# Loading all of w4 as one tile over 16 DMA engines, in place of 128 rows apart, in a decode kernel of attention and MLP

## The chip, the cores, the metric

One core of one Trainium2 chip. The metric is the device time of one execution in microseconds (us); most fast runs of one kernel lie within about 0.3% of each other. A trace of one profiled execution stands beside the times; its span is the time from the first to the last instruction, about 1.8 us less than the time.

## The reference

One decode step for 4 batch entries: attention of 32 query heads over the last 2048 entries of a cache with 16 key/value heads, plus a small MLP, added up.

```python
q = (xn @ wq)                       # [4, 32 heads, 128]
scores = einsum(q, K window) / sqrt(128); p = softmax(scores); o = p @ V window
attention = o @ wo                  # [4, 576]
h2 = gelu(layernorm(x1) @ w3) @ w4  # w3: [576, 4608], w4: [4608, 576]
out = x + attention + x1 + h2
```

K and V windows are 16 x 2 MB each, the weights some 20 MB more: 87 MB are read for an output of 4.5 KB.

## The kernel before

SyncE issues all large loads in one fixed order into one queue. K and V share six buffers; w4 has the buffer of wq and w3. The kernel before holds 35 of 36 w4 rows of each partition in a tile and brings the last 128 rows apart, in eight small loads whose shapes are chosen so that they go to few DMA engines.

```python
NFM = NF - 1                                   # 35
W4_PIECES = [0, NFH, NFM - 11, NFM - 6, NFM - 2, NFM - 1, NFM]
def load_w4():
    t = wp.tile([P, NFM, D], BF16, tag="w", name="w4_sb")
    for lo, hi in zip(W4_PIECES, W4_PIECES[1:]):
        ...
        nc.sync.dma_start(out=t[:, lo:hi, :], in_=src[:, lo - e * NFH:hi - e * NFH, :])

def x4_rows(part):
    t = w_tiles["x4"]                          # a buffer of the K and V pool
    if part == "A":                            # 100 rows: 5 shares of 4 partitions x 5 rows
        src = B_w4[X0 + 28:F, :].rearrange("(q g i) n -> g q (i n)", q=4, g=5)
        nc.sync.dma_start(out=t[0:NX, XA * D:XS * D], in_=src)
    elif part == "C":                          # 12 rows: 3 shares of 4
        ...
    else:                                      # B, 16 rows in six loads of one partition each
        ...
X_AFTER = {13: ["A", (0, 0, 4)], 14: [(1, 0, 4), (2, 0, 2), "C"], 15: [(2, 2, 4), (3, 0, 2), (3, 2, 4)]}
...
order = [("K", 0), ("K", 1), ("K", 2)]         # then V0, K3, V1, K4 ... V13, X, V14, V15; then w4
def flush_loads():                             # issues the next loads while buffers are free
    ...
            if kind == "X" or kind == "V" and h > min(X_AFTER):
                for part in X_AFTER.get(h, []):
                    x4_rows(part)
...
mlp_extra(XC, XS)                              # 12 + 8 matmuls on the rows apart, near the end
...
for lo, hi in pieces:
    mlp_out(lo, hi)                            # two matmuls for each row of the tile
```

## Time and profile before

| | before |
|---|---|
| time, fast runs of the first two series | 211.12 to 211.66 us |
| span of the profiled execution | 209.6 us |
| read from memory | 87.17 MB |
| last completion of V15 / of w4 | 194.51 / 206.60 us |
| first of w4's sixteen completions | 204.81 us |

A load over 16 DMA engines is complete when all sixteen have reported. The trace holds each report, so each load has sixteen completion times, without the number of the engine. They are given below as sorted lists. "Late" is an engine that has been set back by some 1.3 us against the others, "half-late" one that has been set back by some 0.5 to 0.9 us.

### The profile page before, as it was taken

To read this page: it belongs to the slowest core of one execution; us is meant where nothing else is said; L and a number is where in the kernel's file an instruction comes from. 1 tells how busy PE (TensorE), PEld (TensorE's weight loads), DVE (VectorE), ACT (ScalarE), POOL (GpSimd) and SP (SyncE) were. 2 spreads that over 40 slices of the span, in tenths; PEclk is the share of its full clock that TensorE was granted. 3 is DMA by queue.
4 is the path that set the end of the run, shared out by engine and by line. 5 is a ranking of instruction groups with operands and counts; after the bars stand their busy time and mean duration, and the time that the engine had idled before them with its cause. 6 is when DMAs were issued, how large, how long until landed. Compare 5 with 4: busy or idle time off the path is not lost.

```text
span 209.6 us, 2356 instructions
## 1 busy us (share of the span) xinstructions
PE 150.2 (72%) x958; PEld 58.2 (28%) x972; DVE 113.4 (54%) x156; ACT 34.8 (17%) x72; POOL 9.0 (4%) x32
## 2 busy tenths in 40 slices
PE   0357297699590039958998987589697955999693
PEld 0122132233140003213444332234232312343361
DVE  4511877894910083935608889176848390764200
ACT  7612201012010011110222221102111111023100
POOL 4710000000000000000002100000000000000000
PEclk9999589999787555788999999789978796699979
DMA  7999999999999999999999999999999999999992
GB/s 301 400 419 425 425 424 430 438 432 424 434 450 406 427 435 420 443 428 435 428 428 435 419 428 434 435 425 438 428 428 438 415 439 435 416 441 428 432 403 98
DMA packets 6702, 87.31 MB, mean 417 GB/s; under 512 B 758, under 2 KB 1034, under 8 KB 1700
## 3 DMA queue, kind: packets, MB, share of 16 engines
q1 hardware_dynamic: 6684, 87.17, 97.7%
q8 instruction: 7, 0.11, 0.2%
q10 hardware_dynamic: 8, 0.00, 0.0%
q14 instruction: 3, 0.02, 0.0%
HBM read 87.17 MB, written 0.00 MB: 416 GB/s over the span
## 4 chain that ended last, share of the span: by engine, by line
DMA 66%; DVE 15%; PE 14%; ACT 1%; issue 1%; SPq 1%; DVEq 0%; ACTq 0%
DMA kn<-in_A_k_cache_dram 43%; DVE kt L253 12%; DMA vn<-in_A_v_cache_dram 10%; DMA w_sb<-in_B_w_dram 7%; DMA wq_sb<-in_A_wq_dram 6%; PE S L366 5%; PE g_ps L496 2%; PE q_ps L310 2%; PE O L423 1%; PE oT L436 1%; DVE PT L400 1%; PE acc L212 1%; DVE mx L372 1%; PE S L388 1%; ACT E L395 1%
## 5 line engine op out<-in xcount | busy, mean ns | idle before, releaser
L366 PE MATMUL S<-kt,qz 128*128 128x512 bf16 x242 | 76.4, 437 | 32.2 <-DVE kt L253 30.4
L253 DVE STREAM_TRANSPOSE kt<-kn 128x2048 int32<-128x2048 int32 x32 | 73.4, 2297 | 24.3 <-DMA kn<-in_A_k_cache_dram 22.9
L366 PEld LDWEIGHTS <-qz 128*128 128x128 bf16 x256 | 23.5, 106 | 64.3 <-issue 47.7
L423 PE MATMUL O<-vn,PT 128*32 128x512 bf16 x256 | 23.9, 414 | 9.3 <-DMA vn<-in_A_v_cache_dram 9.3
L430 ACT ACTIVATE O_sb<-O,rd 128x512 f32<-128x512 f32 x16 | 11.0, 686 | 64.7 <-DVE rd L413 48.3
L395 ACT ACTIVATE E<-S 128x512 bf16<-128x512 f32 x16 | 9.5, 597 | 72.6 <-PE S L388 72.6
L400 DVE STREAM_TRANSPOSE PT<-E 128x512 bf16<-128x512 bf16 x16 | 11.4, 710 | 14.4 <-ACT E L395 14.4
L446 DVE TENSOR_REDUCE on<-oT 128x8 bf16<-128x128 f32 x16 | 4.6, 289 | 22.1 <-PE oT L436 21.9
L423 PEld LDWEIGHTS <-PT 128*32 128x32 bf16 x256 | 5.5, 95 | 33.0 <-issue 22.1
L436 PE MATMUL oT<-ident_w,O_sb 128*128 128x128 f32 x64 | 12.7, 331 | 0.3 <-ACT O_sb L430 0.3
L372 DVE TENSOR_REDUCE mx<-S 128x1 f32<-128x512 f32 x16 | 10.5, 659 | 1.1 <-PE S L366 1.1
L436 PEld LDWEIGHTS oT<-ident_w,O_sb 128*128 128x128 f32 x64 | 8.3, 165 | 5.2 <-issue 4.3
L388 PE MATMUL S<-nm,j_row 8*128 8x512 bf16 x16 | 6.7, 421 | 1.8 <-DVE nm L384 1.7
L354 PE MATMUL S<-negbig,ohT 4*128 4x512 bf16 x16 | 6.2, 384 | 0.0
L212 PE MATMUL acc<-w_sb,gT 128*4 128x288 bf16 x70 | 5.5, 311 | 0.6 <-DMA w_sb<-in_B_w_dram 0.6
L310 PE MATMUL q_ps<-wq_sb,xnT 128*32 128x512 bf16 x40 | 4.3, 611 | 2.2 <-DMA wq_sb<-in_A_wq_dram 2.2
L212 PE MATMUL acc<-wo_sb,op 128*4 128x288 bf16 x64 | 5.5, 324 | 0.4 <-DVE op L468 0.4
L496 PE MATMUL g_ps<-w_sb,ln2T 128*32 128x512 bf16 (+2 forms) x55 | 5.5, 441 | 0.0
L212 PEld LDWEIGHTS <-gT 128*4 128x4 bf16 (+3 forms) x90 | 4.2, 89 | 3.1 <-issue 1.0
L538 POOL TENSOR_TENSOR g_u<-g_x 128x180 f32<-128x180 f32 x1 | 0.5, 486 | 101.9 <-ACT g_x L532 101.9
L681 DVE CAST fin<-acc 4x288 bf16<-4x288 f32 x1 | 0.4, 446 | 8.1 <-PE acc L212 8.1
L534 DVE COPY g_x<-gT_ps 128x64 f32<-128x64 f32 x2 | 0.4, 223 | 7.5 <-PE gT_ps L518 7.5
(94 smaller groups left out, 79.3 us busy)
## 6 DMA issues: line engine op xcount, KB each, us to landing
kn<-in_A_k_cache_dram SPq DMA_DIRECT2D x16, 2048.0 KB, 25.9
vn<-in_A_v_cache_dram SPq DMA_DIRECT2D x16, 2048.0 KB, 22.7
wo_sb<-in_A_wo_dram SPq DMA_DIRECT2D x4, 1152.0 KB, 37.8
w_sb<-in_B_w_dram SPq DMA_DIRECT2D x1, 4608.0 KB
wq_sb<-in_A_wq_dram SPq DMA_DIRECT2D x1, 4096.0 KB
w_sb<-in_B_w_dram SPq DMA_DIRECT2D x1, 2592.0 KB, 11.0
w_sb<-in_B_w_dram SPq DMA_DIRECT2D x2, 576.0 KB, 34.3
w_sb<-in_B_w_dram SPq DMA_DIRECT2D x1, 864.0 KB
```

The lines of the kernel that those rows point to most:

```text
L212: nc.tensor.matmul(out=acc_of(i), lhsT=lhsT, rhs=rhs[:, i * CW:(i + 1) * CW], start=False, stop=False, skip_group_check=True)
L253: nc.vector.transpose(out=kt[:], in_=src)
L310: nc.tensor.matmul(out=q_ps[r][g * QD:(g + 1) * QD, :], lhsT=xnT[:, k, :], rhs=wq_sb[:, col:col + NW], start=(j == 0), stop=False, skip_gr ...
L366: nc.tensor.matmul(out=S_ps[h][:], lhsT=qz[:, z0:z0 + P], rhs=kt[:, ib, c0:c0 + SC, e:2 * QD:2].rearrange("p c k -> p (c k)"), start=False ...
L372: nc.vector.reduce_max(out=mx[:], in_=S_ps[h][:], axis=AX.X)
L388: nc.tensor.matmul(out=S_ps[h][:], lhsT=j_row[:], rhs=st.pop(("nm", h))[:, 0:1].to_broadcast([NJ, NW]), start=False, stop=False, skip_grou ...
L395: nc.scalar.activation(out=E[h][:].rearrange("p c k -> p (c k)"), in_=S_ps.pop(h)[:], func=ACT.Exp, scale=scale, accum_out=st["rs"][:, h % ...
L400: nc.vector.transpose(out=PT[h][:], in_=E.pop(h)[:])
L423: nc.tensor.matmul(out=O_ps[h][g * QD:(g + 1) * QD], lhsT=PT[h][:, c, :], rhs=vn[:, :, c, :], start=(s == 0), stop=False, skip_group_check ...
L430: nc.scalar.activation(out=O_sb[h][:], in_=O_ps.pop(h)[:], func=ACT.Copy, scale=st.pop(("rd", h)))
L436: nc.tensor.transpose(out=oT[:, s, :], in_=o[:, s, :], identity=ident_w[:, s * NJ:s * NJ + P])
L496: nc.tensor.matmul(out=out, lhsT=ln2T[:, k, :], rhs=rhs, start=(j == 0), stop=False, skip_group_check=True)
```

## The change

It drops the loads apart and all that serves them, for a simpler kernel: one tile of 36 rows, the usual 16 engines, no matmuls on four, twelve or twenty partitions, no reordering of the MLP's columns.

```diff
-    NFM = NF - 1
-    W4_PIECES = [0, NFH, NFM - 11, NFM - 6, NFM - 2, NFM - 1, NFM]
+    W4_PIECES = [0, NFH, NF - 12, NF - 6, NF - 2, NF - 1, NF]
     def load_w4():
-        t = wp.tile([P, NFM, D], BF16, tag="w", name="w4_sb")
+        t = wp.tile([P, NF, D], BF16, tag="w", name="w4_sb")
...
-    def x4_rows(part):
-        ... (parts A, B and C)
-    X_AFTER = {13: ["A", (0, 0, 4)], ...}
...
     # in mlp_g, told in words: out go the matmuls on the 128 columns apart and ACT's copies of them in a new order
     # in mlp_turn, told in words: out go ten transposes and five ACT copies, in comes one DVE copy, as in the other rounds
...
-            if kind == "X":
-                load_x4()
-            else:
-                load_kv(kind, h)
-            ...
+            load_kv(kind, h)
...
-    mlp_extra(XC, XS)
-    mlp_extra(XB, XC)
```

## The prediction

> **What bounds the kernel now.** I read the page's busy slices first, then the chain of waits, then the last 10 us in order of time, then the landing of every transfer. The title of the change also speaks of denominators that two heads share. The kernel before already does that (its step of the denominators returns at even heads), and the diff does not touch it: nothing is counted for it. What changes is w4 alone.
>
> The page, DMA row and rate in 40 slices, and the queue that carries the loads:
> ```profile
> DMA  7999999999999999999999999999999999999992
> GB/s 301 400 419 425 425 424 430 438 432 424 434 450 406 427 435 420 443 428 435 428 428 435 419 428 434 435 425 438 428 428 438 415 439 435 416 441 428 432 403 98
> ...
> q1 hardware_dynamic: 6684, 87.17, 97.7%
> q8 instruction: 7, 0.11, 0.2%
> ```
> All slices but the first and the last are full. 87.17 MB between the first packet (about 1.4 us) and the last landing (206.60 us) are 425 GB/s. Compute shows no such row: PE is busy 72% and DVE 54% of the span.
>
> The end of the chain of waits of the kernel before, and the SyncE issues from 158 us on:
> ```profile
> 167.94 21.71 DMA vn<-in_A_v_cache_dram
> ...
> 191.35 14.53 DMA w_sb<-in_B_w_dram
> 205.88 0.04 issue
> 205.92 1.05 PE acc L212 x12
> 206.97 0.43 DVE fin L681
> ```
> ```profile
> 163.21 0.91 SPq L164 DMA_DIRECT2D x<-in_B_w_dram  x1
> 164.17 0.36 SPq L171 DMA_DIRECT2D x<-in_B_w_dram  x1
> 167.94 0.55 SPq L103 DMA_DIRECT2D vn<-in_A_v_cache_dram  x1
> 168.55 1.91 SPq L171 DMA_DIRECT2D x<-in_B_w_dram  x2
> 175.07 0.82 SPq L167 DMA_DIRECT2D x<-in_B_w_dram  x1
> 179.94 0.56 SPq L103 DMA_DIRECT2D vn<-in_A_v_cache_dram  x1
> 184.76 0.81 SPq L171 DMA_DIRECT2D x<-in_B_w_dram  x3
> 189.67 5.67 SPq L153 DMA_DIRECT2D w_sb<-in_B_w_dram  x6
> ```
> The chain ends with w4's landing, 12 short matmuls, the copy and the store. The 21.71 us on V and the 14.53 us on w4 are mostly queueing: V15, issued at 179.94 us, lands at 194.51, one regular period of 4.86 us after V14 (189.65). Each 2 MB load of K or V lands that far after the one ahead of it through the whole second half. So no issue comes late enough to leave an engine without work, and issuing earlier can gain nothing.
>
> **The sixteen engines apart.** The trace has each engine's completion of each transfer. K2's sixteen lie between 28.23 and 28.74 us. At 30.63 us a packet of 16384 B of the instruction queue runs for 967 ns, and in the next transfer (wo) fifteen engines end between 30.98 and 31.46 us and one at 32.80: 1.34 us behind the next to last. It never catches up; V0 has it at 37.66, K3 at 42.50. Six more such packets come at 64.8, 105.2, 121.7, 147.0, 179.1 and 198.7 us, and after each of those I can follow one more engine is late. V12 ends on eleven engines at 173.14 to 173.97 and on five at 174.60 to 175.06.
>
> The kernel before uses this. It takes the last 128 rows of w4 out of the tile (35 rows instead of 36 for a partition) and loads them apart: part A completes on 5 engines (183.75 to 184.56 us), part C on 3, each of the six pieces of B on one. After the first of these, V14 shows five engines at 187.83 to 188.17 and the rest up to 189.65; at the end w4 has four at 204.81 to 205.14 and twelve at 205.91 to 206.60. Late engines and laden engines were made to end together. They are different engines: a late one with part A's 20 rows on top would have landed V15 about 0.9 us after 194.51, and none does.
>
> **What the Trainium skill says.** "DMA: Bandwidth & Descriptors", section "Why a DMA increments its semaphore by 16 and not by 1": a transfer from SyncE runs on the largest number of engines up to 16 that divides the slowest dimension of both sides, and on the lowest-numbered ones. The trace agrees on the number (5, 3 and 1 completions for slowest dimensions of 5, 3 and 1); which engines they are it cannot show. The same page, "Where 436 GB/s comes from", puts the ceiling at 435 GB/s; the 425 here is close to it, the rest being the imbalance at the end and the start. "Runtime: NRT & Kernel Launch", section "Instruction fetch mechanics": instructions are refilled in 16 KiB blocks, at a cost it calls "mostly hidden". The trace shows the 16384 B packets, hidden from the compute engine indeed, but costing one DMA engine 1.34 us that it never makes up.
>
> **The change, part by part.**
>
> Transfers: removed are eight small loads (2.2 to 112.5 KB, 147,456 B together); added is one row for each partition in the tile, the same 147,456 B over all sixteen engines, 8 rows or 9,216 B each. Per engine this is: one engine loses 40 rows and gains 8, two lose 24, two lose 20, and eleven only gain 8. The last late engine is among those eleven. It took from 194.51 (V15) to 206.60 us for 280 rows of 1152 B, or 322,560 B in 12.09 us, 26.7 GB/s. The 9,216 B more take 9,216 / 26.7 GB/s = 0.345 us (the single-row pieces of w4, 8 rows on an engine, landed 0.36 us apart, 206.24 and 206.60, which agrees). Hence w4's last landing goes from 206.60 to about 206.95 us. This lies wholly on the path that sets the end. The other term, the relief of five engines by 12 to 32 rows (0.5 to 1.4 us), is worth nothing, for nobody waits for them.
>
> PE: 20 short matmuls on x (12 at 193.02 for 0.90 us, 8 at 197.86 for 0.65 us) go, and two on the tile's extra row come, some 0.16 us by the 78 ns spacing of the 58 at 200.78 (4.53 / 58). The 12 run while V15 is awaited (194.65), the 8 beside the DVE pair of mk and op (197.97 to 198.85); neither is on the path. The 2 more fall into the 0.61 us in which PE waited for w4 before 205.92. After the last landing the same two matmuls, copy and store remain: 0 us.
>
> PE, ACT, POOL in the MLP stage at 98 to 116 us: five matmuls, ten transposes and about eight small ACT copies go, one DVE copy of some 0.2 us (223 ns for its larger kin) comes. The loads of that stage kept their 4.85 us period, so this is worth 0 us.
>
> SyncE and buffers: x's place in the order of loads and its eight issues go. V14 can take x's place at 163.2 us, V15 that of V14 at 167.9, and w4's pieces follow between 168 and 185 as their semaphores come free, instead of 189.7 to 194.9 us. They only wait longer in the queue: 0 us.
>
> Sum: +0.345 us. The fast times before are 211.28, 211.57 and, profiled, 211.41, mean 211.42. I expect 211.42 + 0.35 = 211.77, and put 211.8.
>
> **The rivals.**
>
> 1. The engines share one limit, so that only bytes count: then 147 KB moved from five engines to sixteen change nothing, +0.0 us, 211.4. For it: the 425 GB/s near the stated ceiling. Against it: the late engine of 30.6 us stays late for over 150 us while the others run on; had they a common limit, slack would be shared out at the end only.
>
> 2. The earlier issue of V14, V15 and w4 and the lost small packets help: -0.3 to -0.5 us, 211.0. For it: the chain names the issues of w4 at 189.67 to 191.35. Against it: 4.86 us between V14 and V15, no gap.
>
> 3. Instruction refills move. Some 66 fewer PE instructions (35 matmuls and transposes with their weight loads, less 4) put the last refills a few us later, the seventh into w4's rows at about 202 us. If each refill keeps its own engine, the one hit then ends below 206.6 us, no harm. If one fell on an engine that is already late, that engine ends 1.34 us later: some 213.1. Against it: seven refills hit seven different engines as far as I can follow them. If one of the late refills disappears, several late engines remain: no gain.
>
> 4. PE becomes the end: rows up to 30 done by about 205.5 us, 0.7 us before they'd be needed at 206.2. A clock lower by a quarter there would use that up and add some 0.5 us.
>
> **Range and chances.** The likely error is run-to-run scatter (0.29 us between the two fast runs) plus rivals 1 and 2 on the low side, 3 and 4 on the high side: 211.3 to 212.6. 2% are 4.2 us, far beyond every term here, the worst being rival 3. Within 2%: 0.98; faster 0.005; slower 0.015.
>
> **What would show it.** In the changed kernel's trace: V14 and V15 with the late engines at the same times as before (189.65 and 194.51) and the gap of five engines at V14 gone, nine to ten engines early instead of five; w4's last completion near 206.95 with nine or so engines at 205.1 to 205.9; the end of the chain again w4, a dozen acc matmuls, fin; issue of w4 before 186 us; the DMA row still full. Wrong would be: last landing at or below 206.6 (rival 1 or 2), an engine some 1.3 us behind all others (rival 3), PE without idle time ahead of its last matmuls (rival 4), or a K or V landing more than 5 us after the one before it, which would mean that compute does reach the queue.

## The result, and the profile after

| | before | after |
|---|---|---|
| median of six runs | 211.50 us | 211.73 us |
| fast runs | 211.12 to 211.66 us | 211.49 to 212.00 us |
| ratio of the fast runs | | 1.0014, 95% interval 1.0000 to 1.0028 |
| span | 209.6 us | 210.0 us |
| last completion of V14, V15 | 189.65, 194.51 us | 189.71, 194.57 us |
| last completion of w4 | 206.60 us | 206.98 us |

One run of the kernel before, of 646.39 us, is among the six of its median and not among the fast ones; the record does not say what it met. A ratio is the mean time of one kernel's fast runs over that of the other's fast runs of the same rounds, so it is not quite the ratio of the medians. 1.0014 of 211.4 us is 0.3 us: same, by any use one could make of it, and at the edge of what six runs resolve. The trace resolves it better.

The page of the kernel after, DMA row, rate and queues:

```profile
DMA  7999999999999999999999999999999999999991
GB/s 300 399 421 431 434 428 428 428 431 438 454 400 421 432 424 426 447 424 424 440 421 434 437 414 438 431 437 428 426 428 434 429 432 434 428 431 437 419 403 61
...
q1 hardware_dynamic: 6632, 87.17, 97.5%
q8 instruction: 7, 0.11, 0.2%
```

The bytes are the same, the row is as full as before, and there are seven refills still (a refill is a packet of the instruction queue, q8, that fetches instructions). The end of its chain of waits, and the issues of SyncE from 155 us on (start us, duration us, what):

```profile
175.13 31.13 DMA w_sb<-in_B_w_dram
206.26 0.04 issue
206.30 1.06 PE acc L181 x12
207.36 0.43 DVE fin L607
```
```profile
157.43 9.99 SPq L103 DMA_DIRECT2D vn<-in_A_v_cache_dram  x3
167.47 17.67 SPq L141 DMA_DIRECT2D w_sb<-in_B_w_dram  x6
207.87 0.35 SPq L610 DMA_DIRECT2D out_dram<-fin  x1
```

The chain has the same four members at its end, 0.38 us later. w4's pieces are now issued between 167.5 and 185.1 us, up to 22 us earlier than before, and they wait the longer: 31.13 us in the chain in place of 14.53. The last matmuls start 0.38 us later (206.30 for 205.92) and the tail after w4's last landing is the same (2.99 us before, 3.03 us after).

The sixteen completions of w4's last piece, in us, from the trace's records:

```
before  204.81 204.96 205.08 205.14 | 205.91 206.16 206.21 206.34 206.36 206.37 206.40 206.42 206.43 206.50 206.51 206.60
after   205.02 205.04 205.08 205.09 205.24 205.25 205.36 205.78 205.98 | 206.49 206.54 206.59 206.61 206.64 206.68 206.98
```

Twelve engines ended together before. Nine engines are early now, and the seven that refills set back end alone, later than before.

### The profile page after: what moved, and what is told of

Same layout as the page of the kernel before. It is cut to its first block, busy times and chain, and to the rows that moved or that the text cites. A ratio compares the mean times of both kernels' runs of the same rounds, so it can differ in the third digit from the quotient of the medians.

```text
span 210.0 us, 2284 instructions
## 1 busy us (share of the span) xinstructions
PE 145.9 (69%) x939; PEld 55.5 (26%) x939; DVE 113.6 (54%) x157; ACT 34.1 (16%) x64; POOL 8.7 (4%) x31
## 4 chain that ended last, share of the span: by engine, by line
DMA 63%; PE 22%; DVE 11%; ACT 1%; issue 1%; SPq 0%; ACTq 0%
DMA vn<-in_A_v_cache_dram 42%; DMA w_sb<-in_B_w_dram 15%; PE S L335 9%; DVE kt L222 9%; DMA wq_sb<-in_A_wq_dram 6%; PE O L392 3%; PE g_ps L457 2%; PE q_ps L279 2%; PE acc L181 1%; PE S L357 1%; PE oT L405 1%; DVE mx L341 1%; ACT E L364 1%; DVE qz L311 1%; PE gT_ps L469 1%
## 5 line engine op out<-in xcount | busy, mean ns | idle before, releaser
L335 PE MATMUL S<-kt,qz 128*128 128x512 bf16 x256 | 77.4, 432 | 33.7 <-DVE kt L222 32.7
L392 PE MATMUL O<-vn,PT 128*32 128x512 bf16 x256 | 23.3, 405 | 11.1 <-DMA vn<-in_A_v_cache_dram 11.1
L405 PE MATMUL oT<-ident_w,O_sb 128*128 128x128 f32 x64 | 11.4, 305 | 0.3 <-ACT O_sb L399 0.3
L405 PEld LDWEIGHTS oT<-ident_w,O_sb 128*128 128x128 f32 x64 | 7.3, 150 | 4.7 <-issue 3.9
L181 PE MATMUL acc<-w_sb,gT 128*4 128x288 bf16 x72 | 5.0, 285 | 2.2 <-DMA w_sb<-in_B_w_dram 2.2
L181 PE MATMUL acc<-wo_sb,op 128*4 128x288 bf16 x64 | 4.6, 286 | 1.0 <-DVE op L437 1.0
L457 PE MATMUL g_ps<-w_sb,ln2T 128*32 128x512 bf16 (+1 forms) x50 | 4.9, 444 | 0.0
L475 DVE COPY g_x<-gT_ps 128x64 f32<-128x64 f32 (+1 forms) x3 | 0.6, 195 | 7.3 <-PE gT_ps L469 7.3
L206 PE MATMUL tp<-ident_bf,first 4*128 4x4 bf16 x8 | 0.6, 173 | 5.5 <-DVE first L193 5.5
## 6 DMA issues: line engine op xcount, KB each, us to landing
vn<-in_A_v_cache_dram SPq DMA_DIRECT2D x16, 2048.0 KB, 26.7
wo_sb<-in_A_wo_dram SPq DMA_DIRECT2D x4, 1152.0 KB, 26.7
```

The costliest lines, as they stand in the source:

```text
L181: nc.tensor.matmul(out=acc_of(i), lhsT=lhsT, rhs=rhs[:, i * CW:(i + 1) * CW], start=False, stop=False, skip_group_check=True)
L335: nc.tensor.matmul(out=S_ps[h][:], lhsT=qz[:, z0:z0 + P], rhs=kt[:, ib, c0:c0 + SC, e:2 * QD:2].rearrange("p c k -> p (c k)"), start=False ...
L392: nc.tensor.matmul(out=O_ps[h][g * QD:(g + 1) * QD], lhsT=PT[h][:, c, :], rhs=vn[:, :, c, :], start=(s == 0), stop=False, skip_group_check ...
L405: nc.tensor.transpose(out=oT[:, s, :], in_=o[:, s, :], identity=ident_w[:, s * NJ:s * NJ + P])
L457: nc.tensor.matmul(out=g_ps[g * QD:(g + 1) * QD], lhsT=ln2T[:, k, :], rhs=rhs, start=(j == 0), stop=False, skip_group_check=True)
```

## The experiments

The theory: each DMA engine works off its own share at its own pace, an engine that fetched instructions stays late for good, and the latest engine sets the end. Rows apart go to engines that have time, so in the tile they cost what they add to the late engines. The main rival: all engines share one limit, and only bytes count.

### Without the rows apart, and with one row less in the tile

Both take 147,456 B away. The first, from the kernel before, takes them off the few engines that carry them; the second, from the kernel after, takes 9,216 B off each of sixteen.

```diff
 # e1_no_rows_apart, on before (wrong on purpose: the matmuls on these rows take rows of wo)
-                for part in X_AFTER.get(h, []):
-                    x4_rows(part)
+                pass
```

> The kernel before, without the eight loads of the rows apart (its matmuls on them stay, on other data, so the result is wrong on purpose). 147,456 B fewer come from memory. My theory (each of the sixteen DMA engines works off its own share, and the engines delayed by instruction refills end last): the engines that carried those rows were not the last, so w4's last completion stays at 206.5 to 206.7 us in the trace and the time stays within 0.1 us of the kernel before. Rival (one common limit, only bytes count): 147,456 B at 425 GB/s are 0.35 us, so the last completion falls to about 206.25 and the time by 0.35 us.

```diff
 # e3_row_35_left_out, on after (wrong on purpose: row 34 used twice)
-    W4_PIECES = [0, NFH, NF - 12, NF - 6, NF - 2, NF - 1, NF]
+    W4_PIECES = [0, NFH, NF - 12, NF - 6, NF - 3, NF - 2, NF - 1]
+    acc_matmuls([(gT[:, NF - 1, :], w_tiles["w4"][:, NF - 2, :])])
```

> The changed kernel with only 35 of the 36 rows of each partition loaded (row 34 is used twice in the products, so the same number of matmuls and a wrong result on purpose). The same 147,456 B fewer, but 9,216 B on each of the sixteen engines. My theory: the last completion of w4 falls by 0.345 us, from 206.98 to about 206.63, and the time by 0.35 us to that of the kernel before. Rival (one common limit): the same 0.35 us; it is the pair with the run without the rows apart that tells the two apart. Rival (the time of the change came from the matmuls or from the order of the loads): nothing changes, 0.0 us.

Measured: the first 211.16 us (ratio to before 0.9986, interval 0.9972 to 0.9999), the second 211.38 us (1.0003, 0.9984 to 1.0021). The second fits the time of the kernel before, as expected, but its interval (0.34 us less to 0.44 us more) would hold the change's 0.3 us as well. The first is at 0.02 to 0.59 us less, an interval that reaches from my "within 0.1" to the rival's 0.35 and beyond. So the times decide neither; the traces do. From V15 to w4 no rows apart are in the queue, and the last engine takes:

| kernel | rows in the tile | last of V15 | last of w4 | between |
|---|---|---|---|---|
| before | 35 | 194.51 | 206.60 | 12.09 |
| e1, no rows apart | 35 | 194.30 | 206.36 | 12.06 |
| e3, row 35 left out | 35 | 194.60 | 206.67 | 12.07 |
| after | 36 | 194.57 | 206.98 | 12.41 |
| e6, empty slot (below) | 36 | 194.50 | 206.87 | 12.37 |
| e7, more PE instructions (below) | 36 | 194.22 | 206.64 | 12.42 |

One row for each partition is 0.33 us, in six executions. For the rows apart one has to look from before they come: the five engines that are late at V12 report at 174.60 to 175.06 us in the kernel before, 174.54 to 174.65 us in e1. The last of them ends w4 31.54 us later in the kernel before (206.60), and in e1 the five end at 206.08 to 206.19 us, 31.54 us later as well; under one limit they'd have 0.35 us less. The mean of the sixteen engines does lose it: from K14 to w4 39.76 us (166.25 to 206.01) before, 39.37 us (166.04 to 205.41) in e1. So the bytes left, and only engines that nobody waits for ended earlier. The 0.2 us by which e1's trace is ahead of that of before (its w4 ends at 206.36 us, just below my 206.5 to 206.7) were there at V12 already, ahead of any row apart; where they come from stays open.

### Later issue again

```diff
 # e6_empty_slot, on after
+        if h == 13:
+            order.append(("X", h))       # takes a K/V buffer, loads nothing
```

> The changed kernel with a buffer of the K and V pool taken and left empty where the kernel before loaded its rows apart, so that V14, V15 and w4 are issued late again (V14 near 168 us instead of 163). My theory: the queue is never empty, so the landings of V14 and V15 (189.71, 194.57 us) and of w4 (206.98) stay within 0.1 us, and the time as well. Rival (the earlier issue of these loads pays back part of what the rows cost): the last completion moves up by 0.2 us or more.

Measured: 211.57 us, ratio 1.0004 (0.9991 to 1.0018); last completions 189.68 (V14), 194.50 (V15), 206.87 us (w4), within 0.11 us of the kernel after. Its issues:

```profile
159.74 13.43 SPq L103 DMA_DIRECT2D vn<-in_A_v_cache_dram  x3
173.23 11.94 SPq L141 DMA_DIRECT2D w_sb<-in_B_w_dram  x6
```

V14 and V15 were issued at 166.66 and 172.64 us, 3.4 and 5.8 us later than in the kernel after (w4's first piece 5.8 us), and nothing landed later. It is not the whole of the old lateness: V15 and w4's first piece still went out 7.3 and 16.4 us earlier than in the kernel before, and for the rest the landings of V14 and V15 before and after must speak (point 1 below). The earlier issue is worth nothing, as long as the queue has work.

### Three more loads on the engine that carries most

```diff
 # e2_engine0_laden, on before: 14 rows into an unused partition, at three places
                 for part in X_AFTER.get(h, []):
                     x4_rows(part)
+                q = 40 + h
+                nc.sync.dma_start(out=w_tiles["x4"][q:q + 1, 0:14 * D],
+                                  in_=B_w4[0:14, :].rearrange("(q i) n -> q (i n)", q=1))
```

> The kernel before with three more loads of 14 rows each into one unused partition, 48,384 B, all on the one engine that already carries 40 rows apart. My theory: that engine alone gets 42 x 43 ns = 1.8 us more; it ended w4 somewhere between 205.9 and 206.6 us, so the last completion goes to 207.7 to 208.4 and the time up by 1.1 to 1.8 us, with the other fifteen completions unmoved. Rival (one common limit): 48,384 B at 425 GB/s are 0.11 us, all completions move by that.

Measured: 214.39 us, ratio 1.0140 (1.0124 to 1.0157), that is +3.0 us. w4's completions: fifteen at 204.89 to 206.72 us, one at 209.22. The end of the chain of waits:

```profile
195.87 12.62 DMA w_sb<-in_B_w_dram
208.49 0.04 issue
208.53 1.06 PE acc L212 x12
209.59 0.43 DVE fin L684
```

48,384 B, 0.06% of all bytes, cost 1.4% of the time because they sit on one engine: the rival's 0.11 us is out. My own size was too small: the three loads took this engine 1.18, 1.01 and 0.88 us (from the completion ahead of each to its own), 3.07 us together, where 26.7 GB/s make 1.8 us. These loads of one partition ran at some 60% of the engine's pace (1.8 of 3.07 us); why, no run here shows. The same trace also places this engine in the kernel before: from its last row apart (197.49) to its end of w4 (209.22) it took 11.73 us, so with its last row apart at 194.66 it ended at about 206.39 us, with the late engines.

### Which engines are late

```diff
 # e5_probes, on after: loads of one row for each of k partitions, behind V13, V14 and V15
 # (a K/V buffer is taken for them after V13, as in e6)
+                for k in {13: (6, 7), 14: (8, 9, 10), 15: (11, 12, 13)}[h]:
+                    nc.sync.dma_start(out=w_tiles["x4"][0:k]..., in_=B_w4[0:k, :])
```

> The changed kernel with eight loads of one row of 1152 B for each of 6, 7, 8, ... 13 partitions behind V13 (6, 7), V14 (8, 9, 10) and V15 (11, 12, 13), in the same queue. Completion counts of 6, 7, ... 13 engines are expected. If a load of k rows runs on the k lowest-numbered engines, its completions tell how late engines 0 to k-1 are, and the difference between k and k-1 tells where engine k-1 stands. My theory: engines 0 to 4 are not among the late ones (the kernel before put its rows apart there), the seven late ones lie among 5 to 15. If instead late ones are among the first five, the kernel before could not have ended at 206.6. Time: engines that carry all eight probes get 8 x 43 ns = 0.35 us more, so 212.0 to 212.2.

Measured: 212.08 us (two runs), and completion counts 6 to 13 as expected. The lists, in us:

```
k = 6   182.91 182.99 183.05 | 183.71 183.84 | 184.60
k = 7   183.08 183.09 183.18 183.23 | 183.88 184.02 | 184.80
k = 10  188.21 188.34 188.38 188.47 188.53 188.56 188.70 | 189.36 189.41 | 190.15
k = 13  193.60 193.62 193.72 193.74 193.78 193.78 194.14 | 194.60 194.67 195.08 195.09 195.16 | 195.74
```

The first five are three early and two half-late ones: part A in the kernel before showed the same, three completions at 183.75 to 183.88 us and two at 184.40 and 184.56. The sixth is late. The seventh to tenth are early. The eleventh to thirteenth add three more to the slow ones. Six were late at V13, so two more are among the last three. The trace has no engine numbers; that the set for k lies within the set for k + 1 is taken from the Trainium skill ("DMA: Bandwidth & Descriptors", section "Why a DMA increments its semaphore by 16 and not by 1": such a transfer runs on the lowest-numbered k engines), and the lists agree with it.

So the kernel before loaded the five engines it could reach without touching a late one, and left some four early ones unused.

Where the half-late engines come from the trace shows too. The kernel after has two packets of 8192 B on queue 14 between its first load and its last, at 49.0 and 149.5 us, and in the loads next to end, K4 and V10, one more engine is some 0.7 to 0.9 us behind its place (51.56 and 151.80 us).

### Part A over ten engines

Nine of the first ten engines have time. Does a wider spread pay?

```diff
 # e8_a_over_ten, on before (result right; the columns of the MLP are reordered alike)
-            src = B_w4[X0 + 28:F, :].rearrange("(q g i) n -> g q (i n)", q=4, g=5)
+            src = B_w4[X0 + 28:F, :].rearrange("(q g i) n -> g q (i n)", q=2, g=10)
```

> The kernel before with part A of the rows apart (100 rows) over ten completions instead of five, 10 rows on each; parts B and C as they were, and the result right. From the probes I take it that the sixth of the engines (the one that loads of 6 rows have and loads of 5 have not) is one of the late ones and the seventh to tenth are not. Theory: the first five engines are relieved by 10 rows (0.43 us), four idle ones take 10 rows at no cost, and the sixth, already late, gets 10 rows more: its completion of w4 moves some 0.43 us behind where the late engines end now, to 206.8 to 207.0, the time up by 0.2 to 0.4 us. Rival (a better spread over more engines pays): the last completion falls to about 206.3 and the time by 0.2 us. Rival (one common limit): nothing moves.

Measured: 212.50 us, ratio 1.0044 (1.0029 to 1.0060), +0.9 us: worse, and worse than expected. w4's completions end with a group at 206.98 to 207.09 us and two at 207.47 and 207.50. The two, 0.4 us behind the group, are 10 rows' worth (0.43 us): one fits the sixth engine, the other an early engine that took 10 rows and was then hit by the refill at 198.8 us. But the whole group of late engines stands 0.5 us behind that of before, and it fell back between K15 and V13, where they took 5.5 us in place of 4.86 (179.60 to 179.73, then 185.08 to 185.26). They carry none of part A but for the sixth. So two more runs:

```diff
 # e10_ten_adjacent and e9_ten_every_fourth, on before (wrong on purpose), 10 shares of 9 rows
+            src = B_w4[X0 + 28:X0 + 118, :].rearrange("(g i) n -> g (i n)", g=10)
+            nc.sync.dma_start(out=t[0:10,   XA * D:(XA + 9) * D], in_=src)   # e10
+            nc.sync.dma_start(out=t[0:40:4, XA * D:(XA + 9) * D], in_=src)   # e9
```

> The kernel before with part A as one load of 10 x 9 rows into ten adjacent partitions, 0 to 9 (the matmuls on the rows apart take other data, so the result is wrong on purpose). It asks what the 0.5 us are by which all late engines of the run with A over ten were set back between K15 and V13. Theory: engines that write into the same few partitions at once disturb each other and the loads beside them; ten engines in partitions 0 to 9 do it at least as much as in 0 to 19, so V13 of the late engines comes 5.3 us or more after K15 (4.86 in the kernel before), w4 ends at 207.2 to 207.9 and the time is 0.5 to 1.3 us above the kernel before. Rival (a disturbance of that one execution): 4.86 us, w4 ends near 207.0 by the sixth engine's rows alone (9 x 43 ns), the time 0.2 to 0.4 us up.

> As the run with ten adjacent partitions, but the ten shares of 9 rows go to partitions 0, 4, 8, ... 36. Theory of crowding in a few partitions: spread like this no more than two shares meet where the others go, V13 of the late engines comes within 5.0 us of K15, w4 ends near 207.0 (the sixth engine's 0.39 us alone) and the time is 0.2 to 0.4 us above the kernel before. Rival (the number of ten shares, or the place in the queue, is what disturbs): the same 0.5 us setback as with adjacent partitions.

Measured: adjacent 212.59 us (1.0057, 1.0030 to 1.0084), every fourth 211.67 us (1.0013, 0.9989 to 1.0037). The late engines took 6.0 to 6.2 us from K15 to V13 with adjacent partitions and 5.05 with every fourth (I had said within 5.0). The stretch in which part A runs, 178 to 186 us, of before, e8, e10 and e9 in this order (PE, PEld, DVE, ACT and POOL busy, granted clock, DMA share, GB/s):

```profile
178.00:186.00 8.00, 7.93 (x48) 2.81 (x49) 6.74 (x8) 0.71 (x2) 0.00 (x0) 0.77 1.00 427
```
```profile
178.00:186.00 8.00, 7.30 (x45) 2.73 (x45) 6.78 (x9) 0.69 (x1) 0.00 (x0) 0.82 1.01 390
```
```profile
178.00:186.00 8.00, 6.98 (x42) 2.29 (x41) 6.79 (x9) 0.69 (x1) 0.00 (x0) 0.77 1.01 358
```
```profile
178.00:186.00 8.00, 7.94 (x50) 2.96 (x52) 6.37 (x9) 0.69 (x1) 0.00 (x0) 0.71 1.02 429
```

The DMA share is full in all four, the rate is not: ten shares into ten adjacent partitions cost 16% of it over these 8 us, or 1.3 us, two partitions a share 9%, every fourth partition nothing that the rate shows, though the late engines still took 0.19 us more than the 4.86 of the kernel before. e9 and e10 differ in the destination alone. The 0.5 us were thus no accident of one execution but crowding at the destination. The Trainium skill has the likely reason: "SBUF — State Buffer", section "Door 1: The DMA port swizzle", puts each four adjacent partitions on one port for DMAs. Part A's four partitions a share in the kernel before fit that, and its window shows no loss (427 GB/s). The ports as such no run shows. With most of the crowding gone, e9 ends at 206.69 us (I had said near 207.0), its two last engines 0.3 us behind the others (206.35). They fit the two of e8: the sixth engine with its rows, last already in V15 (194.68), and one that joins it after the refill at 198.75 us. It is no better than the kernel before (206.60), and no version here beats that one. In e10, the profiled execution was the slowest of four (213.48 us), and there PE came last, with 81 matmuls on acc in 8.26 us at the end of the chain; its w4 landed at 208.16 us, 0.3 us above my range.

### More instructions for PE

```diff
 # e7_pe_refill_more, on after, while PE waits for wq
+    for _ in range(130):
+        nc.tensor.matmul(out=idle[0:B, 0, 0:B], lhsT=ident_bf[:, 0:B], rhs=ident_bf[:, 0:B], start=True, stop=True)
```

> The changed kernel with 130 tiny matmuls (and their weight loads, some 260 PE instructions) while PE waits for the first weights, before 16 us; nobody reads their result. PE's instruction refills[...] all come earlier by about one block: the first already before 20 us, eight instead of seven in all. Theory: a first late engine shows already in the landings before 30 us (in the changed kernel the first comes with the refill at 30.4), six instead of five engines are late at V12 (around 173 us), eight at the end. If the eighth falls on an engine not yet late, w4 still ends within 0.2 us of 206.98; if on a late one, near 208.3. Rival (the lateness comes from something else at those times, not from refills): the first late engine still appears between 28.5 and 32.6 us and five are late at V12.

Measured: 211.45 us, ratio to before 0.9998 (0.9985 to 1.0011). The page:

```profile
q8 instruction: 8, 0.13, 0.2%
```

Eight refills, the first at 17.0 us. In the next landing, K0, fifteen engines report at 18.37 to 18.92 us and one at 20.09; in the kernel after, K0 has all sixteen at 18.27 to 18.77 and the first late one comes in the landing of wo (32.61 against 31.24 for the next), with the refill at 30.4. At V12 six are late (174.56 to 174.78), at the end eight (206.44 to 206.64). The late engines follow the refills: shift those and they shift. The eighth found an engine that was not yet late. w4 ends at 206.64 us, 0.34 us earlier than in the kernel after (I had said within 0.2), though each row costs the same (12.42 us from V15 to w4, table above): here the latest engine lies 1.57 us behind the first, in the kernel after 1.96. There the spread jumped from 1.60 to 2.11 us with the refill at 105.3 us, which must have hit an engine that was a little behind already. Which engine a refill hits is thus worth as much as this whole change, and no run here controls it.

### Refills for GpSimd

```diff
 # e4_pool_refills, on after, behind mlp_act
+                    for _ in range(1100):
+                        nc.gpsimd.memset(junk[:], 0.0)
```

> The changed kernel with 1100 tiny writes on GpSimd after its part of the MLP stage, into a tile nobody reads; GpSimd is idle then. They need instruction refills of their own: 1100 x 64 B are 4.3 blocks of 16384 B, so three to five more such packets between 116 and 209 us. My theory (each refill costs one DMA engine some 1.3 us of its share for good): after each, one more engine is late in the next landing. If they fall on engines not yet late, more than seven engines are late at the end and w4's last completion stays near 207.0 (time +0.0 to 0.2 us). If one falls on an engine already late, that one ends 1.3 us behind all others, w4 near 208.3 and the time +1.3 us. Rival (the lateness has another cause than the refills): the number of late engines stays at seven and the time as well.

Measured: 291.0 us, ratio 1.3745. As a timing it failed: the writes came one every 158 ns (1100 between 115.7 and 289.2 us) and GpSimd itself became the end.

```profile
L568 POOL MEMSET junk<- 128x2 f32 x1100 | 110.4, 100 | 63.1
```
```profile
q8 instruction: 7, 0.11, 0.1%
q14 instruction: 12, 0.10, 0.1%
```

The loads were done by 207.80 us and can still be read. GpSimd's refills are other packets than I expected, 8192 B on queue 14, some 20.3 us or 129 writes apart (8192 / 129 is 63.5 B a write), five between 116 and 209 us: 120.9, 141.2, 161.9, 181.6 and 202.1. At the end eight engines are late (206.42 to 207.80), in the kernel after seven. The eighth joins between V11 and K14: six late in place of five at K14 (166.92 to 167.32), after the packet at 161.9 us, with none of PE's refills near (147.8 and 181.7). The packet at 181.6 us came 0.15 us ahead of PE's refill. Of the seven engines that were early at K15 (177.81 to 178.00), six were so at V13 (182.70 to 182.85), and a new one was the last there, at 185.10, 0.53 us behind the next. With both on one engine, that is what one would see. In w4's first piece this engine was 0.47 us behind the next, in the second, after the packet at 202.1, 1.10. w4 ended 0.8 us later than in the kernel after, on that engine alone (206.76 is the next). So refills make engines late here too, and a second one on the same engine does move the end, which is the third rival of the prediction at work; by how much in time this run cannot say.

## Why the prediction was right

Point by point, by its own steps.

1. *The queue bounds the kernel, and issue order is worth nothing.* Right: V14 and V15 of the kernel after landed within 0.06 us of before though issued 4.7 and 13.1 us earlier, and e6 showed the same from the other side.
2. *Refills make engines late for good.* Right, and shown by moving them (e7). The 1.34 us read from the first one is a typical size; e7's first was 1.17 (20.09 against 18.92), the kernel after's 1.37, each against the next engine.
3. *Late and laden engines are different ones, and the late ones set the end.* Right: e5 finds late engines from the sixth on, and e1's late engines do not move when the rows apart go.
4. *The term of 0.345 us.* Measured as 0.33 (12.40 less 12.07 on the mean of three executions each), w4's end 206.98 us for the 206.95 predicted.
5. *The relief of five engines is worth nothing.* Right: in the kernel after nine engines end at 205.02 to 205.98 us and wait. For the engine that carried part B the relief was larger than the 43 ns a row that the prediction took, if its loads of one partition ran as slowly as those of e2; it made no difference.
6. *PE's and ACT's savings are worth nothing.* Right: PE waited 1.09 us for w4 ahead of its row 24 and 0.48 us ahead of row 30; its busy time fell from 150.2 to 145.9 us and the time rose.
7. *The sum.* Forecast 211.8, measured 211.73 us. That the sum hit so close owes something to luck: runs of the kernel after spread by 0.5 us, those of the kernel before in one later series by 1.0 us, and e7 shows a shift of 0.3 us by a refill's place alone, a term that the forecast had only in its range. e6 and e7 load the same 36 rows and measured ratios of 1.0004 and 0.9998 to the kernel before, with intervals that reach from below 0 to 0.4 and 0.2 us. In time the cost of the change is thus not resolved; in the traces it is (point 4).

Of the rivals, the common limit is out (e2, e1's trace); the earlier issue too (e6); a second refill on one engine exists (e4) but did not strike this change in that form; PE as the end was seen once, in the profiled execution of e10.

## What to carry to other kernels

When the load queue is full from end to end, ask which engine is the last and what that one carries; bytes taken from the others gained nothing here (e1), and bytes added to it were paid in full, at one engine's pace (0.33 us for a row of each partition) or slower (e2). The completions of each load, sixteen for one, show it where the mean rate shows nothing. A small load cut into many shares should also spread its destination partitions: ten shares into ten adjacent ones took the rate of all engines together to 358 GB/s, into every fourth it stayed at 429.

## What the Trainium skill lacked or had wrong

- "Runtime: NRT & Kernel Launch", section "Instruction fetch mechanics", calls the cost of a refill mostly hidden. It lacks that the 16384 B packet runs 0.88 to 1.00 us on one DMA engine and sets it back by 1.2 to 1.4 us for the rest of the kernel (three first refills, each against the next engine: 1.17, 1.34, 1.37 us), which is paid in a kernel bound by its loads.
- The same section gives blocks of 16 KiB. PE's refills were 16384 B here; GpSimd's came as 8192 B packets, one for some 129 writes (e4).
- "DMA: Bandwidth & Descriptors" lacks the pace of a load of one partition: 16,128 B took its engine 0.88 to 1.18 us, against 0.60 us at the 26.7 GB/s of its share in a load over 128 partitions (e2).
- The same page and "SBUF — State Buffer", section "Door 1: The DMA port swizzle", lack a number for what crowding costs the other loads in the queue: ten shares into ten adjacent partitions took the rate of all engines from 427 to 358 GB/s over 8 us, into every fourth partition none that the rate shows (429 GB/s).
